# Sums one at a time, and one line of product steps across block borders, in a fused attention and SwiGLU kernel

## The chip, the cores and the metric

The kernel runs on one core of one Trainium2 chip. Time is device time in microseconds (us) of one execution. Before the change the median of 13 runs is 353.88 us, from 352.03 to 356.42.

## The reference

Sliding-window attention with an ALiBi bias feeds a SwiGLU block. The attention has 8 batches, 8 heads, 576 positions, 64 values per head and a window of 128. Its output is laid out as a matrix x of 4608 tokens by 512. Then:

```
attn = softmax(scale * q @ k.T + bias, masked to the window) @ v
x    = attn, as [4608, 512]
g    = x @ w_gate                     # [4608, 1536]
h    = g * sigmoid(g) * (x @ w_val)   # [4608, 1536]
out  = h @ w_out                      # [4608, 512]
```

Inputs and output are float32; the kernel computes its products in float16 with float32 sums.

## The kernel before, in words

**Blocks.** The tokens go in nine blocks (0 to 8) of 512. A block's x is held transposed (`xT`, four chunks of 128 rows by 512 tokens), and so is its h (`hT`, twelve chunks of 128 rows by 512 tokens). Attention runs beside blocks 0 to 5 and is finished before block 6, so blocks 6 to 8 and the tail hold only the SwiGLU part. The change lies there.

**h @ w_out by seven products.** `strassen(n, t)` computes the output of block n for one half of its tokens, t = 0 or 1, as a 2x2 block product with seven multiplications instead of eight (the Winograd form). Its operands are quarters of `hT` and three sums of them, S2, S3 and S4 (a fourth sum, S1, is written over a quarter of `hT`). Each of the seven steps is one product of six matmuls (line 525), followed by a copy on ScalarE or by a scaled add into an output row (`osb`) on VectorE (line 529). The 14 steps of a block, t = 0 and then t = 1, are called p0 to p13 here. The third and tenth (p2, p9) read S2, the fifth and twelfth (p4, p11) S3, the sixth and thirteenth (p5, p12) S4. S2, S3 and S4 have one buffer each (pool `sp`). The accumulators X and Y of a `strassen` are the two halves of one PSUM tile with one buffer.

**The sums of h.** `sums(n, c)` makes a third of S2, S3 and S4, from the chunks of units c and c + 3, in four operations on VectorE: S3, the in-place add, S2, S4 (lines 492 to 495).

**Gate and value by seven products.** For blocks 6 to 8 (`SEVEN_FROM` is 6) `gate_val_by_seven(n)` computes gate and value with the same form. It works on six units of 256 gate columns each. A unit has seven steps, named first to seventh, each a product of four matmuls (line 617). On PSUM tiles X, Y and Z: first starts X, and ScalarE copies it to Z; fifth starts Y (copied as p5); sixth adds to X (copied as u2); second adds to Z, and ScalarE takes its silu; third adds to Y, VectorE adds u2 (line 653) and multiplies into `hT` (line 654); seventh adds to X, VectorE adds p5 (line 660), which gives v; fourth adds to X after that, ScalarE takes its silu (line 667), and VectorE multiplies it with v into `hT` (line 668). X and Y come from a pool of four PSUM banks. x has sums too: `x_sums(n)` makes three of them and one in place (lines 600 to 603), in halves of the masks' memory that attention has left.

**Order of the steps.** A unit's steps are mixed with those of the unit ahead of it:

```
for step, of in ((first, u), (seventh, u - 1), (fifth, u), (sixth, u), (fourth, u - 1),
                 (second, u), (third, u)):
```

The loop runs to u = 6, so the last unit's seventh and fourth come alone at the end of the block, before the next block begins. After every third step one h product of the block before is put in (`parts`). After the last block, `ends` emits the fourteen h products of block 8 in a written order.

**What sets the order on the engines.** From step 198 of the emission on, TensorE runs in the order in which the program is written; VectorE's and ScalarE's order is chosen by a planner from its own estimates, and each runs its queue in that order. SP's queue holds the transposes of x and the stores of output rows; POOL's queue holds the loads, all done by then.

Of the kernel before, what the change touches and what calls it, by code (L numbers as in the profile page):

```python
# [31 lines left out]
SEVEN_FROM = 6  # L32
SILU_AT = 7
# [18 lines left out]
def kernel(  # L52
# [10 lines left out]
    nc = tc.nc  # L63
# [4 lines left out]
    NMB = DFF // P  # L68
    NSUP = B // 2
    NBLK = NTOK // 512  # L70
# [93 lines left out]
    units = [(s, p) for s in range(NSUP) for p in range(9)]  # L164
# [265 lines left out]
    def gate_val(n, m):  # L430
        c0 = 384 if (n, m) in acted else 0
        gate(n, m, wide(n, m, "g"), c0)
        yield
        val(n, m, wide(n, m, "v"), c0)
        yield
# [45 lines left out]
    one_more = []  # L481
    hsum = {}

    def sums(n, c):

        if n not in hsum:
            hsum[n] = [spool.tile([P, HM, 256], FP16, name=f"S{i}", tag=f"S{i}") for i in (2, 3, 4)]
        lo, hi = slice(2 * c, 2 * c + 2), slice(HM + 2 * c, HM + 2 * c + 2)
        a11, a12 = hT[n][:, lo, 0:256], hT[n][:, hi, 0:256]
        a21, a22 = hT[n][:, lo, 256:512], hT[n][:, hi, 256:512]  # L490
        s2, s3, s4 = (t_[:, lo, :] for t_ in hsum[n])
        nc.vector.tensor_sub(s3, a11, a21)
        nc.vector.tensor_add(a21, a21, a22)
        nc.vector.tensor_sub(s2, a21, a11)
        nc.vector.tensor_sub(s4, a12, s2)

    def strassen(n, t):

# [75 lines left out]
    G1, G2 = wg_sb[:, 0:HK, :], wg_sb[:, HK:NKB, :]  # L574
    V1, V2 = wv_sb[:, 0:HK, :], wv_sb[:, HK:NKB, :]
# [10 lines left out]
    def gate_val_weight_sums(u):  # L586

        cols = slice(2 * u * P, (2 * u + 2) * P)
        t1, t2, t3, t4 = tsum[u] = t_homes[4 * u:4 * u + 4]
        nc.vector.tensor_sub(t1, V1[:, :, cols], G1[:, :, cols])  # L590
        nc.vector.tensor_sub(t3, V2[:, :, cols], V1[:, :, cols])
        nc.vector.tensor_sub(t2, V2[:, :, cols], t1)
        nc.vector.tensor_sub(t4, G2[:, :, cols], t2)

    def x_sums(n):

        a11, a12 = xT[n][:, 0:HK, 0:256], xT[n][:, HK:NKB, 0:256]
        a21, a22 = xT[n][:, 0:HK, 256:512], xT[n][:, HK:NKB, 256:512]
        s2, s3, s4 = xsum[n] = spare[3 * (n % 2):3 * (n % 2) + 3]
        nc.vector.tensor_sub(s3, a11, a21)  # L600
        nc.vector.tensor_add(a21, a21, a22)
        nc.vector.tensor_sub(s2, a21, a11)
        nc.vector.tensor_sub(s4, a12, s2)

    def gate_val_by_seven(n):

        x = xT[n]
        A11, A12 = x[:, 0:HK, 0:256], x[:, HK:NKB, 0:256]
        S1, A22 = x[:, 0:HK, 256:512], x[:, HK:NKB, 256:512]
        S2, S3, S4 = xsum.pop(n)  # L610
        hT[n] = hpool.tile([P, NMB, 512], FP16, name="hT", tag="hT")
        live = {}

        def product(dst, w, c0, a, start=False):
            for i in range(2):
                for kb in range(HK):
                    nc.tensor.matmul(dst[:, i, :], w[:, kb, c0 + i * P:c0 + (i + 1) * P], a[:, kb, :],  # L617
                                     start=(start and i == 0 and kb == 0),
                                     stop=(i == 1 and kb == HK - 1), skip_group_check=True)

        def first(u):
            X, Y = (ps_a.tile([P, 2, 256], FP32, name=i, tag="a", bufs=4) for i in ("gX", "gY"))
            Z = ps_f.tile([P, 2, 256], FP32, name="gZ", tag="gv")
            live[u] = X, Y, Z
            product(X, G1, 2 * u * P, A11, True)
            nc.scalar.copy(Z, X)

        def fifth(u):
            Y = live[u][1]
            product(Y, tsum[u][0], 0, S1, True)  # L630
            p5 = epool.tile([P, 2, 256], FP32, name="p5", tag="exc", bufs=5)
            nc.scalar.copy(p5, Y)
            live[u] += (p5,)

        def second(u):
            Z = live[u][2]
            product(Z, G2, 2 * u * P, A12)
            s = supool.tile([P, 2, 256], FP16, name="s1", tag="tt")
            nc.scalar.activation(s, Z, AF.Silu)
            live[u] += (s,)  # L640

        def sixth(u):
            X = live[u][0]
            product(X, tsum[u][1], 0, S2)
            u2 = epool.tile([P, 2, 256], FP32, name="u2", tag="exc", bufs=5)
            nc.scalar.copy(u2, X)
            live[u] += (u2,)

        def third(u):
            X, Y, Z, p5, u2, s = live[u]  # L650
            product(Y, V2, 2 * u * P, S4)
            v_ = supool.tile([P, 2, 256], FP16, name="v1", tag="uu")
            nc.vector.tensor_add(v_, Y, u2)
            nc.vector.tensor_mul(hT[n][:, 2 * u:2 * u + 2, 0:256], s, v_)

        def seventh(u):
            X, Y, Z, p5, u2, s = live[u]
            product(X, tsum[u][2], 0, S3)
            v_ = supool.tile([P, 2, 256], FP16, name="v2", tag="uu")
            nc.vector.tensor_add(v_, X, p5)  # L660
            live[u] = X, v_

        def fourth(u):
            X, v_ = live.pop(u)
            product(X, tsum[u][3], 0, A22)
            s = supool.tile([P, 2, 256], FP16, name="s2", tag="tt")
            nc.scalar.activation(s, X, AF.Silu)  # L667
            nc.vector.tensor_mul(hT[n][:, 2 * u:2 * u + 2, 256:512], s, v_)  # L668

        last_u = NMB // 2  # L670
        for u in range(last_u + 1):
            for step, of in ((first, u), (seventh, u - 1), (fifth, u), (sixth, u), (fourth, u - 1),
                             (second, u), (third, u)):
                if 0 <= of < last_u:
                    step(of)
                    if step is fourth and of >= last_u // 2:
                        sums(n, of - last_u // 2)
                    yield step

    AT = {2, 3, *range(5, 10), *range(11, 18)}  # L680

    def ffn():

        for n in range(NBLK):
            if n > 1:
                parts = chain(strassen(n - 1, 0), strassen(n - 1, 1))
            if n == 1:
                for j in range(PRE):
                    for _ in project(0, j, ps_f, "po", 1):
                        yield 1.0  # L690
            if n >= SEVEN_FROM:
                k = 0
                for k, _ in enumerate(gate_val_by_seven(n)):
                    if n == SEVEN_FROM and k in (3, 10, 17):
                        gate_val_weight_sums(3 + k // 7)
                    yield 0.5
                    if k % 3 == 1 and next(parts, 0) is None:
                        yield 0.75
                    if k == 36 and n + 1 < NBLK:
                        x_sums(n + 1)  # L700
                assert next(parts, 0) == 0
                continue
            for m in range(NMB):
                for half, _ in enumerate(gate_val(n, m)):
                    yield 1.0
                    if n > 1 and 2 * m + half in AT:
                        next(parts)
                        yield 0.75
                if n == 1:
                    if m in (4, 6, 8, 10):  # L710
                        for _ in project(0, m // 2 - 2, ps_f, "po", 1):
                            yield 1.0
                    if m in (4, 6, 8):
                        weight_sums(m // 2 - 2)
                if n > 0 and m >= 9:
                    sums(n, m - 9)
                if n + 1 == SEVEN_FROM:
                    if m == SILU_AT:
                        attention_ends()
                        by_silu.update((n, i) for i in range(m + 1, NMB))  # L720
                    if m in (SILU_AT + 1, SILU_AT + 2):
                        gate_val_weight_sums(m - SILU_AT - 1)
                    if m == NMB - 1:
                        gate_val_weight_sums(2)
                        x_sums(n + 1)
            if n > 1:
                assert next(parts, 0) == 0

        ends = [strassen(NBLK - 1, t) for t in range(2)]
        for t in (0, 1, 0, 1, 0, 0, 0, 1, 0, 0, 1, 1, 1, 1):  # L730
            next(ends[t])
            yield 0.75

# [220 lines left out]
```

## Time and profile before

| | |
|---|---|
| median of 13 runs | 353.88 us |
| lowest, highest | 352.03, 356.42 us |
| the profiled execution: its time, its span | 354.86 us, 353.1 us |
| TensorE busy, matmuls | 336.1 us (95%), 2983 |
| VectorE busy, instructions | 277.6 us (79%), 652 |
| ScalarE busy, instructions | 207.1 us (59%), 412 |
| mean granted TensorE clock | 0.990 |
| block 6 begins; last product of block 8's fourth begins | 249.19 us; 339.43 us |

The page has the busy time of each engine, the span in 40 slices of 8.83 us with the busy share of each in tenths, and groups of instructions by line. Besides it the trace answers who waited for whom, and lists the instructions of one engine in order of time. In such a list a line has the start in us, the duration in us, the engine, the line of the kernel, the operation, and output<-input with shapes; a wait before it stands in brackets with the instruction that ended it. PE is TensorE, DVE is VectorE, ACT is ScalarE. Line numbers are those of the kernel before.

### The profile page before, as it was taken

To read this page: it belongs to the slowest core of one execution; us is meant where nothing else is said; L and a number is where in the kernel's file an instruction comes from. 1 tells how busy PE (TensorE), PEld (TensorE's weight loads), DVE (VectorE), ACT (ScalarE), POOL (GpSimd) and SP (SyncE) were. 2 spreads that over 40 slices of the span, in tenths; PEclk is the share of its full clock that TensorE was granted. 3 is DMA by queue.
4 is the path that set the end of the run, shared out by engine and by line. 5 is a ranking of instruction groups with operands and counts; after the bars stand their busy time and mean duration, and the time that the engine had idled before them with its cause. 6 is when DMAs were issued, how large, how long until landed. Compare 5 with 4: busy or idle time off the path is not lost.

```text
span 353.1 us, 7803 instructions
## 1 busy us (share of the span) xinstructions
PE 336.1 (95%) x2983; PEld 221.0 (63%) x2983; DVE 277.6 (79%) x652; ACT 207.1 (59%) x412; POOL 108.2 (31%) x134
## 2 busy tenths in 40 slices
PE   7999989999999999999999999999999799799975
PEld 3584445444456655666566655566788688688864
DVE  5568886999787799778998999999756955845673
ACT  2758773566555756656556554474666567476630
POOL 8966584348485564545310000000000000000000
PEclk9999998999999999999999999999999999989999
DMA  9999999999999999999995032123010101101014
GB/s 151 170 180 186 141 183 161 93 141 130 141 166 179 155 180 158 178 142 188 170 125 106 18 90 17 42 64 90 2 61 0 61 3 59 62 0 61 0 61 120
DMA packets 158981, 37.37 MB, mean 106 GB/s; under 512 B 147296, under 2 KB 154592, under 8 KB 158944
## 3 DMA queue, kind: packets, MB, share of 16 engines
q0 software_dynamic: 117280, 18.62, 77.9%
q1 hardware_dynamic: 40976, 17.64, 28.0%
q10 hardware_dynamic: 688, 0.62, 0.6%
q8 instruction: 23, 0.38, 0.5%
q14 instruction: 14, 0.11, 0.1%
HBM read 37.91 MB, written 9.44 MB: 134 GB/s over the span
## 4 chain that ended last, share of the span: by engine, by line
PE 70%; DVE 18%; ACT 4%; DMA 4%; issue 3%; POOL 0%; ACTq 0%; DVEq 0%
PE po L525 14%; PE pg L398 13%; PE pv L398 13%; PE gX L617 7%; PE gY L617 4%; PE ps L279 4%; PE av L346 3%; PE po L452 3%; DMA qn<-in_q_dram 3%; PE p L525 3%; DVE hT L428 2%; DVE uu L417 2%; PE gZ L617 2%; ACT ex L285 2%; PE pt L222 1%
## 5 line engine op out<-in xcount | busy, mean ns | idle before, releaser
L398 PE MATMUL pv<-xT,wv_sb 128*128 128x512 f16 (+2 forms) x320 | 76.8, 358 | 0.4 <-DVE hT L428 0.2
L398 PE MATMUL pg<-xT,wg_sb 128*128 128x512 f16 (+2 forms) x320 | 76.2, 358 | 0.4 <-DVE hT L428 0.2
L416 ACT ACTIVATE tt<-pg 128x512 f16<-128x512 f32 (+2 forms) x70 | 41.5, 592 | 39.6 <-PE pg L398 39.0
L285 ACT ACTIVATE ex<-ps 128x512 f16<-128x512 f32 x96 | 50.5, 606 | 16.3 <-PE ps L279 16.3
L417 DVE SCALAR_TENSOR_TENSOR uu<-tt,pg 128x512 f16<-128x512 f16 (+2 forms) x69 | 45.9, 665 | 11.1 <-ACT tt L416 11.0
L428 DVE TENSOR_TENSOR hT<-uu,pv 128x512 f16<-128x512 f16 (+2 forms) x70 | 46.5, 664 | 3.4 <-PE pv L398 1.8
L398 PEld LDWEIGHTS <-wg_sb 128*128 128x128 f16 x320 | 28.5, 98 | 25.2 <-issue 3.5
L525 PEld LDWEIGHTS <-hT 128*128 128x128 f16 x384 | 36.9, 99 | 11.4 <-issue 3.0
L398 PEld LDWEIGHTS <-wv_sb 128*128 128x128 f16 x320 | 28.5, 98 | 24.5 <-issue 2.7
L191 POOL DMA_DIRECT2D kn<-in_k_dram x39 | 33.3, 857 | 33.1 <-DMA kT<-kn 24.8
L191 POOL DMA_DIRECT2D qn<-in_q_dram x39 | 33.3, 858 | 24.5 <-DMA qT<-qn 7.6
L185 POOL DMA_DIRECT2D va<-in_v_dram x40 | 34.1, 858 | 21.7 <-PE av L346 16.9
L291 DVE TENSOR_TENSOR ex<-ex,m_reg 128x1024 f16<-128x1024 f16 x42 | 28.8, 687 | 5.6 <-ACT ex L285 5.4
L525 PEld LDWEIGHTS <-S 128*128 128x128 f16 x288 | 27.5, 98 | 7.6 <-issue 1.8
L349 DVE TENSOR_TENSOR x<-av,rec 128x256 f16<-128x256 f32 x72 | 28.8, 419 | 0.5
L525 PE MATMUL po<-T,hT 128*128 128x256 f16 x192 | 26.2, 273 | 1.4 <-DVE osb L529 1.4
L668 DVE TENSOR_TENSOR hT<-s,v 128x512 f16<-128x512 f16 x18 | 7.6, 423 | 24.7 <-ACT s L667 24.7
L525 PE MATMUL po<-T,S 128*128 128x256 f16 x192 | 26.1, 273 | 0.3 <-ACT p5s L553 0.3
L318 ACT ACTIVATE exc<-psc 128x512 f16<-128x512 f32 x40 | 21.4, 610 | 7.6 <-PE psc L314 7.6
L346 PEld LDWEIGHTS <-ex 128*128 128x128 f16 x384 | 17.8, 98 | 5.2 <-issue 0.9
L346 PE MATMUL av<-va,ex 128*128 128x65 f16 x384 | 19.7, 194 | 0.3
L279 PE MATMUL ps<-qT,kT 64*128 64x256 f16 x192 | 18.4, 272 | 0.6 <-DVE osb L529 0.2
(134 smaller groups left out, 540.8 us busy)
## 6 DMA issues: line engine op xcount, KB each, us to landing
out_dram<-osb SPq DMA_DIRECT2D x32, 256.0 KB, 2.4
va<-in_v_dram POOLq DMA_DIRECT2D x32, 128.0 KB, 9.3
qn<-in_q_dram POOLq DMA_DIRECT2D x31, 128.0 KB, 7.6
kn<-in_k_dram POOLq DMA_DIRECT2D x31, 128.0 KB, 7.7
wo_sb<-in_moe_w_out_dram POOLq DMA_DIRECT2D x2, 768.0 KB, 9.7
wg_sb<-in_moe_w_gate_dram POOLq DMA_DIRECT2D x4, 256.0 KB, 7.9
wv_sb<-in_moe_w_val_dram POOLq DMA_DIRECT2D x4, 256.0 KB, 8.3
wg_sb<-in_moe_w_gate_dram POOLq DMA_DIRECT2D x1, 512.0 KB, 9.2
```

What stands on the lines that cost most here:

```text
L185: nc.gpsimd.dma_start(va[rank][p0:p1, :, 0:D], src)
L191: nc.gpsimd.dma_start(t_[p0:p1], src)
L279: nc.tensor.matmul(two[par][:, j, :], kT[rows, ks, pair, :], qT[rows, p:p + 2, pair, :], start=(j == 0 and not early_tile), stop=(j == 1))
L285: nc.scalar.activation(e[:, o:o + 2, :], banks[q4][par], AF.Exp, scale=scale)
L291: nc.vector.tensor_mul(e[:, o, :], e[:, o, :], reg[:, o, :])
L346: nc.tensor.matmul(av[:, j, :], w, val, start=(n == 0), stop=(n == len(todo) - 1))
L398: nc.tensor.matmul(ps[:, c0:c1], w[:, kb, ms], xT[n][:, kb, c0:c1], start=(kb == 0 and c0 == 0), stop=(kb == NKB - 1 and c1 == 512), skip_ ...
L416: nc.scalar.activation(tt, pg[:, c0:c1], AF.Tanh, scale=0.5)
L417: nc.vector.scalar_tensor_tensor(out=uu, in0=tt, scalar=one if (n, m) == PIN else 1.0, in1=pg[:, c0:c1], op0=ALU.add, op1=ALU.mult)
L428: nc.vector.tensor_mul(hT[n][:, m, c0:c1], acted[(n, m)][1][:, c0:c1], pv[:, c0:c1])
L525: nc.tensor.matmul(dst, a[:, m, cols], b[:, m, :], start=(start and m == 0), stop=(m == HM - 1), skip_group_check=True)
L617: nc.tensor.matmul(dst[:, i, :], w[:, kb, c0 + i * P:c0 + (i + 1) * P], a[:, kb, :], start=(start and i == 0 and kb == 0), stop=(i == 1 an ...
```

## The change

The sums of h, of x and of the weights are no longer emitted in fours on the spot. The functions return lists of single operations; in blocks 6 to 8 these go into a list `later`, from which one or two are emitted behind each product step. Outside of that stretch `at_once` emits them as before. The sums of x for the next block are put on the list at step 20 of a block instead of behind step 36.

The steps of the three blocks' eighteen units form one line, `seven_steps`. A block's last unit does its seventh and fourth between the steps of the next block's first unit. In the last unit of block 8, seventh comes behind second, and the first h product of the tail is put behind it. The h products of a block are counted from its step 0, one behind every third step; those of block 6's predecessor begin at the same count.

```diff
+    def four_sums(a11, a12, a21, a22, s2, s3, s4):
+
+        return [lambda: nc.vector.tensor_sub(s3, a11, a21),
+                lambda: nc.vector.tensor_add(a21, a21, a22),
+                lambda: nc.vector.tensor_sub(s2, a21, a11),
+                lambda: nc.vector.tensor_sub(s4, a12, s2)]
+
+    def at_once(fs):
+        for f in fs:
+            f()
+
     def sums(n, c):
 ...
-        nc.vector.tensor_sub(s3, a11, a21)
-        nc.vector.tensor_add(a21, a21, a22)
-        nc.vector.tensor_sub(s2, a21, a11)
-        nc.vector.tensor_sub(s4, a12, s2)
+        return four_sums(a11, a12, a21, a22, s2, s3, s4)
 ...
-        last_u = NMB // 2
-        for u in range(last_u + 1):
-            for step, of in ((first, u), (seventh, u - 1), (fifth, u), (sixth, u), (fourth, u - 1),
-                             (second, u), (third, u)):
-                if 0 <= of < last_u:
-                    step(of)
-                    if step is fourth and of >= last_u // 2:
-                        sums(n, of - last_u // 2)
-                    yield step
+        return {f.__name__: f for f in (first, second, third, fourth, fifth, sixth, seventh)}
+
+    def seven_steps():
+
+        units = [(n, u) for n in range(SEVEN_FROM, NBLK) for u in range(NMB // 2)]
+        of = {}
+        for i, (n, u) in enumerate(units):
+            if u == 0:
+                of[n] = gate_val_by_seven(n)
+            now, before = (n, u), units[i - 1] if i else None
+            if i + 1 < len(units):
+                turn = (("first", now), ("seventh", before), ("fifth", now), ("sixth", now),
+                        ("fourth", before), ("second", now), ("third", now))
+            else:
+                turn = (("first", now), ("seventh", before), ("fifth", now), ("sixth", now),
+                        ("fourth", before), ("second", now), ("seventh", now), ("third", now),
+                        ("fourth", now))
+            for k, (name, which) in enumerate(turn):
+                if which is not None:
+                    of[which[0]][name](which[1])
+                yield n, 7 * u + k, name, which
 ...
-            if n >= SEVEN_FROM:
-                k = 0
-                for k, _ in enumerate(gate_val_by_seven(n)):
-                    if n == SEVEN_FROM and k in (3, 10, 17):
-                        gate_val_weight_sums(3 + k // 7)
-                    yield 0.5
-                    if k % 3 == 1 and next(parts, 0) is None:
-                        yield 0.75
-                    if k == 36 and n + 1 < NBLK:
-                        x_sums(n + 1)
-                assert next(parts, 0) == 0
-                continue
+            if n == SEVEN_FROM:
+                break
 ...
         ends = [strassen(NBLK - 1, t) for t in range(2)]
-        for t in (0, 1, 0, 1, 0, 0, 0, 1, 0, 0, 1, 1, 1, 1):
+        final = ()
+        for n, k, name, which in seven_steps():
+            if k == 0 and n > SEVEN_FROM:
+                assert next(parts, 0) == 0
+                parts = chain(strassen(n - 1, 0), strassen(n - 1, 1))
+            if n == SEVEN_FROM and k in (3, 10, 17):
+                later.extend(gate_val_weight_sums(3 + k // 7))
+            yield 0.5
+            if k % 3 == 1 and k < 42:
+                next(parts)
+                yield 0.75
+            if k == 20 and n + 1 < NBLK:
+                later.extend(x_sums(n + 1))
+            if k == 35:
+                later.extend(sums(n, 0))
+            if name == "fourth" and which is not None and which[1] > 3:
+                if which == (NBLK - 1, 5):
+                    at_once(final)
+                else:
+                    later.extend(sums(which[0], which[1] - 3))
+            if n == NBLK - 1 and k == 40:
+                final = sums(n, 2)
+                later.append(final.pop(0))
+            for _ in range(2 if len(later) > 4 or k >= 39 or k < 7 else 1):
+                if later:
+                    later.pop(0)()
+            if n == NBLK - 1 and k == 41:
+                next(ends[0])
+                yield 0.75
+        assert next(parts, 0) == 0 and not later
+
+        for t in (1, 0, 1, 0, 0, 0, 1, 0, 0, 1, 1, 1, 1):
             next(ends[t])
             yield 0.75
```

More of the change, by code (lines that the diff above doesn't have):

```diff
@@ L589, in gate_val_weight_sums @@
         t1, t2, t3, t4 = tsum[u] = t_homes[4 * u:4 * u + 4]
[L590 to L593, printed above, removed]
+        return [lambda: nc.vector.tensor_sub(t1, V1[:, :, cols], G1[:, :, cols]),
+                lambda: nc.vector.tensor_sub(t3, V2[:, :, cols], V1[:, :, cols]),
+                lambda: nc.vector.tensor_sub(t2, V2[:, :, cols], t1),
+                lambda: nc.vector.tensor_sub(t4, G2[:, :, cols], t2)]
     def x_sums(n):
@@ L599, in x_sums @@
         s2, s3, s4 = xsum[n] = spare[3 * (n % 2):3 * (n % 2) + 3]
[L600 to L603, printed above, removed]
+        return four_sums(a11, a12, a21, a22, s2, s3, s4)
+    later = []
     def gate_val_by_seven(n):
@@ L649, in third @@
         def third(u):
-            X, Y, Z, p5, u2, s = live[u]
+            X, Y, Z, p5, u2, s = live[u][:6]
             product(Y, V2, 2 * u * P, S4)
@@ L660, in seventh @@
             nc.vector.tensor_add(v_, X, p5)
-            live[u] = X, v_
+            live[u] += (v_,)
         def fourth(u):
-            X, v_ = live.pop(u)
+            X, v_ = live[u][0], live[u][-1]
+            del live[u]
             product(X, tsum[u][3], 0, A22)
@@ L715, in ffn @@
                 if n > 0 and m >= 9:
-                    sums(n, m - 9)
+                    at_once(sums(n, m - 9))
                 if n + 1 == SEVEN_FROM:
@@ L721, in ffn @@
                     if m in (SILU_AT + 1, SILU_AT + 2):
-                        gate_val_weight_sums(m - SILU_AT - 1)
+                        at_once(gate_val_weight_sums(m - SILU_AT - 1))
                     if m == NMB - 1:
-                        gate_val_weight_sums(2)
-                        x_sums(n + 1)
+                        at_once(gate_val_weight_sums(2))
+                        at_once(x_sums(n + 1))
             if n > 1:
```

## The prediction

> **What bounds the kernel now.** I read the page's shares first, then the waits of the stretch that the change touches (249 to 353.1 us, blocks 6 to 8 and the tail), then the two engines' timelines at a border between blocks.
>
> The page, shares and slices:
>
> ```profile
> PE 336.1 (95%) x2983; PEld 221.0 (63%) x2983; DVE 277.6 (79%) x652; ACT 207.1 (59%) x412; POOL 108.2 (31%) x134
> ...
> PE   7999989999999999999999999999999799799975
> PEld 3584445444456655666566655566788688688864
> DVE  5568886999787799778998999999756955845673
> ```
>
> TensorE is the bound, full except in slices 31, 34 and 38. Those lie where block 6, 7 and 8 end, and VectorE is at 9, 8 and 7 there against 4 to 6 in the middle of a block. The waits of the stretch, as us in total, times, longest:
>
> ```profile
> DVE hT L668 <- ACT s L667: 24.7, 14, 2.0
> ...
> PE gX L617 <- DVE v L660: 4.2, 3, 1.4
> ...
> PE po L525 <- DVE osb L529: 1.4, 3, 0.5
> ```
>
> TensorE waits six times in 104 us, twice at each of three places, always for VectorE. The first line says that VectorE has slack inside a block (up to 2.0 us per unit), so only the borders cost. TensorE's timeline at the end of block 6, and VectorE's beside it:
>
> ```profile
> 274.74 0.60 PE L617 MATMUL gY<-m_reg,wv_sb 128*128 128x256 f16 x4
> 275.17 0.60 PE L617 MATMUL gX<-m_reg,m_c 128*128 128x256 f16 x4
> 276.22 0.81 PE L525 MATMUL po<-T,hT 128*128 128x256 f16 x6 [0.45 <-DVE osb L529]
> 278.43 0.60 PE L617 MATMUL gX<-xT,m_c 128*128 128x256 f16 x4 [1.39 <-DVE v L660]
> 278.86 0.60 PE L617 MATMUL gX<-xT,wg_sb 128*128 128x256 f16 x4
> ```
>
> ```profile
> 271.01 0.69 DVE L653 TENSOR_TENSOR v<-gY,u 128x512 f16<-128x512 f32 x1 [0.42 <-PE gY L617]
> ...
> 275.76 0.41 DVE L529 SCALAR_TENSOR_TENSOR osb<-po,u2s 128x256 f32<-128x256 f32 x1
> ...
> 277.69 0.68 DVE L660 TENSOR_TENSOR v<-gX,p 128x512 f16<-128x512 f32 x1
> ```
>
> An x product (4 matmuls) takes 0.437 us from start to start (275.17 less 274.74), an h product (6 matmuls) 0.656. So seventh of unit 5 ends at 275.61 and the h product starts 0.61 late; that one ends at 276.88 and fourth starts 1.55 late. Together 2.16 us. VectorE runs without a gap from 271.01 to 278.7, and the v that fourth waits for is only reached at 277.69. Blocks 7 and 8 repeat both waits (305.89 and 308.09; 337.23 and 339.43), so the borders hold 3 x 2.16 = 6.48 us. After block 7 there is more:
>
> ```profile
> 308.09 0.95 PE L617 MATMUL gX<-xT,m_c 128*128 128x256 f16 x4 [1.39 <-DVE v L660]
> 308.83 1.06 PE L617 MATMUL gX<-xT,wg_sb 128*128 128x256 f16 x4
> 309.69 1.06 PE L617 MATMUL gY<-xT,kT 128*128 128x256 f16 x4
> 310.54 1.35 PE L525 MATMUL po<-wo_sb,hT 128*128 128x256 f16 x6
> 311.72 0.60 PE L617 MATMUL gX<-m_reg,kT 128*128 128x256 f16 x4
> ```
>
> The same four products took 278.43 to 280.39, 1.96 us, after block 6, and 3.63 us here: 1.67 us lost to a slower clock, at one border of three.
>
> [...] while fourth waits, nothing behind it runs. [...] seventh's result was there at about 275.8, and v was reached at 277.69. [...] two gaps of 0.61 and 1.55 us were enough once, and not enough twice.
>
> **The change, part by part.** No instruction is added or removed on any engine; the queues of SP and POOL keep their order, so no DMA moves.
>
> Single sums. TensorE alone is ordered by hand here; VectorE's order is the planner's. At a border it is nearly what it was: the same 17 operations stand between v of third(4) and v of seventh(5), three S3 sums still together. I cost this part alone at nothing. What is new: the first half of an output row (osb from p5s) moves ahead of two of them, and add, S2 and S4 of the last group are now mixed with the next block's v.
>
> One line across borders. Now fourth(5) comes three steps behind seventh(5), as inside a block, with p0, fifth and sixth of the next block between. The h products move one place against the unit's steps, one in every three steps as before. I went through the waits inside a block. The tightest are a copy or output row (0.2 us after the product, 0.34 to 0.60 long) against three steps (1.31 us) to its next user, and fourth, which needs v of seventh within 1.53 us and gets it after 0.2 + 0.7. The trace shows no wait for the same pairs today. Cost nothing; without that cover about 0.4 us for each of 18 units.
>
> Now the border. I count from the end of third(4), 270.81 in the trace. TensorE without a stall: p11 to 0.66, first(5) 1.09, seventh(4) 1.53, fifth 1.97, p12 2.62, sixth 3.06, fourth(4) 3.50, second 3.93, p13 4.59, third(5) 5.03, next first 5.46, seventh(5) 5.90, p0 6.56, fifth 6.99, sixth 7.43, and fourth(5) is due. VectorE needs the same 6.68 us as in the trace (271.01 to 277.69), from 0.20: v begins at 6.88, and with its 0.68 and 0.05 for the signal TensorE goes on at 7.62. A stall of **0.19**. p13 is due at 3.93; the osb that it waits for starts about 3.1 and ends at 3.6, so the 0.61 goes.
>
> What is late next is p2 of the next block, which reads S2. In the kernel before, S2's last third was ready at 281.25 and used at about 284.1. Now p2 follows fourth(5) after p1, second, third and first: 0.656 + 3 x 0.437 = 1.97 us, and its fifth weight load is the first to read the last third, at 10.47 with the 0.19. VectorE at the border 6 to 7: v 6.88 to 7.48, then the four x sums that the planner puts here (0.45 each, since each waits for the last) until 9.2, hT of fourth (silu ends at fourth's end + 0.83 = 8.89) 9.2, osb 9.5, add 9.85, v of the next third 10.2, S2 from 10.8 to 11.2. Stall **0.80**. Border 7 to 8 has no x sums: hT 8.89, osb 9.23, add 9.56, v 9.90, S2 10.50 to 10.92, stall **0.51**. Behind p2 wait seventh and fifth of the new block, and nothing else is late.
>
> The tail. Unit 5 has no next block, so seventh(5) moves up behind p13 and one of the tail's products behind it. v now stands one v, one sum and one product earlier: it begins at 5.59 and ends at 6.28, fourth is due at 6.12, stall **0.22**. Three h products instead of four lie before S2's first user: due at 9.19, S2 ends at 9.22, **0.09**.
>
> Sum: 6.48 - (0.19 + 0.80) - (0.19 + 0.51) - (0.22 + 0.09) = **4.5 us** less. Against the profiled execution, 354.86: 350.4. If the border's clock drop goes with the stall, another 1.67: 348.7. The median, 353.88, is 0.98 lower; 13 runs spread over 4.4 us while the border stalls repeat to 0.01, so I read the spread as more or fewer clock drops, and give the median run 0.6 us of them at borders. 353.88 - 4.5 - 0.6 = **348.8**.
>
> Bounds of what the trace doesn't show: the two S2 waits, 0 (if the planner's order leaves more slack than I count) to 1.5 each (if v or silu come 0.7 later); I take 0.80 and 0.51, counted from measured pitches. The clock: 0 to 3 drops of 1.67 are saved, or one new one is bought.
>
> **The rivals.**
> VectorE keeps up: no stall left at the borders. All of 6.48 and the clock share: 346.8. For it, up to 2.0 us of slack per unit; against it, the dense stretch from 271.01 to 278.7 keeps its operations and order.
> The lag only moves: VectorE is the bound at a border, and p2 takes most of what fourth gives. If S2 comes 0.8 later than I count at each of the three places and the clock drops stay, the gain is 4.5 - 2.4 = 2.1: 351.8. For it, the waits computed above; against it, 2 us of slack in the very next unit.
> The change doesn't do what it says: the planner undoes the single emission, as its order already shows. Then the second part alone acts, which is the forecast, not another time.
> Slower: p2 becomes a worse place to wait than fourth was. Place: the last third of S2, three x products behind fourth(5). Each us by which it comes later than I count costs a us at each border. At 1.5 us later (S2 waits of 2.3, 2.0 and 1.6) the 4.5 are gone, at 2.1 the kernel is 1.8 slower: 355.7. 1.5 us is five more sums (0.34) or three more v (0.60) in front of S2; the order has none, so only late inputs (silu, p5) could do it.
>
> **How the numbers follow.** Forecast 0.56 (own range 347.2 to 350.6), VectorE keeps up 0.18, the lag moves 0.18, slower 0.08. The range from 346.3 to 352.3 leaves out the slow case and the outer ends. A measurement of this kernel tells about 0.5% from no change, 1.8 us. Faster by that (under 352.1): the first two and over half of the third, 0.85; within it the rest of the third, 0.08; slower 0.07.
>
> **What would show it.** Right: fourth's wait for v at 0.0 to 0.4, three times; the wait of the h product for osb gone; a new wait of TensorE for the S sum behind the borders after block 6 and 7, the first longer; slices 31, 34 and 38 of TensorE at 9 nearly throughout; matmul counts unchanged. Wrong: waits of TensorE inside blocks, for a copy or for osb; S2 waits over 1.5; or half-clock stretches at places where there were none.

## The result, and the profile after

The changed kernel takes **348.91 us** (median of 11 runs, 348.0 to 349.35) against 353.93 for the kernel before beside it (48 runs, 351.96 to 356.63). The ratio is 0.985, with a 95% interval from 0.9825 to 0.987: faster by 1.5%. The profiled execution took 349.35 us, its span 347.6.

The page of the changed kernel, shares and slices (a slice is 8.69 us here):

```profile
PE 333.9 (96%) x2983; PEld 219.4 (63%) x2983; DVE 277.5 (80%) x652; ACT 207.4 (60%) x412; POOL 108.2 (31%) x134
...
PE   7999988999999999999999999999999999999995
...
PEclk9999999999999999999999999999999999999999
```

The numbers of instructions are the same. Counted from 0 as in the prediction, TensorE's slices stand at 9 from slice 7 to slice 38: the three dips of before (slices 31, 34 and 38) are filled. From the first product of block 6 to the last product of the tail it was 99.21 us (249.19 to 348.40) and is 93.55 (249.25 to 342.80).

Who waits for whom in that stretch, as us in total, times, longest:

```profile
DVE hT L676 <- ACT s L675: 21.4, 13, 1.9
...
PEld L533 <- DVE S L488: 1.8, 3, 0.9
PE po L533 <- DVE S L488: 1.0, 2, 0.6
PE gX L624 <- DVE v L667: 0.6, 3, 0.2
```

Lines have moved: 624 is the x product, 533 the h product, 667 seventh's v, 488 the sum S2. TensorE's wait for an output row (`osb`) is gone. Its wait for v has shrunk from 4.2 to 0.6, and the sum S2 is a new releaser, seen by the weight load first and then by the product behind it. This view counts from the listed end of a product (277.85 + 0.60 below, which leaves 0.17), so I measure waits as before, from the pitch of the products (0.437, which leaves 0.33). The changed kernel's TensorE at the border after block 6:

```profile
277.85 0.60 PE L624 MATMUL gX<-m_reg,kT 128*128 128x256 f16 x4
278.62 0.60 PE L624 MATMUL gX<-xT,m_c 128*128 128x256 f16 x4 [0.17 <-DVE v L667]
279.06 0.82 PE L533 MATMUL p<-wo_sb,hT 128*128 128x256 f16 x6
279.71 0.60 PE L624 MATMUL gZ<-xT,wg_sb 128*128 128x256 f16 x4
280.15 0.60 PE L624 MATMUL gY<-m_c,wv_sb 128*128 128x256 f16 x4
280.59 0.60 PE L624 MATMUL gX<-xT,wg_sb 128*128 128x256 f16 x4
281.02 0.60 PE L533 MATMUL po<-T,S 128*128 128x256 f16 x4
282.27 0.39 PE L533 MATMUL po<-T,S 128*128 128x256 f16 x2 [0.65 <-DVE S L488]
```

Fourth of unit 5 comes at 278.62, 0.33 after the end of sixth (277.85 + 0.437). Then p1, second, third and first of the new block run without a gap, and p2 stops before its fifth matmul: four matmuls from 281.02 end at 281.46, the fifth starts at 282.27, 0.81 late. After block 7 the same two are 0.34 and 0.50, in the tail 0.37 and 0.10. Together 2.45 us where 6.48 stood, and no other product waits between 249 and 343 us.

The chain of waits of the changed kernel, cut to that border, says who holds the end here:

```profile
277.97 0.60 DVE v L667
278.57 0.34 DVE m_reg L486
...
280.20 0.42 DVE hT L676
280.61 0.33 DVE osb L548
280.95 0.33 DVE hT L487
281.28 0.60 DVE v L660
281.88 0.34 DVE S L488
282.22 0.05 issue
282.27 0.39 PE po L533 x2
```

After block 6 VectorE works off its queue without a gap, with x sums (lines 486 to 489) between v and the multiply, and TensorE starts 0.05 us after S2's last third. The lag of VectorE is still there. What changed is that TensorE has other work while it lasts.

After block 7, where no x sums stand in the queue, the second wait has a longer chain. VectorE is idle before the multiply until fourth's silu is there:

```profile
306.55 0.68 DVE L667 TENSOR_TENSOR v<-gX,p 128x512 f16<-128x512 f32 x1
308.55 0.43 DVE L676 TENSOR_TENSOR hT<-s,v 128x512 f16<-128x512 f16 x1 [1.32 <-ACT s L675]
```

So a late v delays fourth, fourth its silu, and the silu the multiply and all that stands behind it in VectorE's queue, up to S2 at 310.16. Half an output row and a v, 0.34 and 0.60 us, stand in that queue ahead of S2, which needs neither. An estimate from these starts: without them, and with 0.45 us from each of the dependent operations to the next, S2 would start at 309.45, 0.7 us sooner, where TensorE waits 0.50. That was not tried.

### The profile page after: what moved, and what is told of

Read it like the earlier page. It is cut to its first block, busy times and chain, and to the rows that moved or that the text cites. A ratio compares the mean times of both kernels' runs of the same rounds, so it can differ in the third digit from the quotient of the medians.

```text
span 347.6 us, 7798 instructions
## 1 busy us (share of the span) xinstructions
PE 333.9 (96%) x2983; PEld 219.4 (63%) x2983; DVE 277.5 (80%) x652; ACT 207.4 (60%) x412; POOL 108.2 (31%) x134
## 4 chain that ended last, share of the span: by engine, by line
PE 59%; DVE 17%; DMA 11%; POOL 4%; issue 4%; ACT 4%; POOLq 0%; ACTq 0%; DVEq 0%
PE po L533 13%; PE pg L398 12%; PE pv L398 11%; PE gX L624 6%; DMA va<-in_v_dram 3%; DMA wo_sb<-in_moe_w_out_dram 3%; PE gY L624 3%; PE av L346 3%; DMA wv_sb<-in_moe_w_val_dram 3%; PE ps L279 2%; PE p L533 2%; DVE hT L428 2%; PE po L452 2%; DMA qn<-in_q_dram 2%; DVE uu L417 2%
```

## The experiments

Besides the changed kernel itself, each kernel is an edit of it. "Stretch" is from the first product of block 6 to the last product of the tail in the profiled run: 93.55 us for the changed kernel, and 93.54 in a second profile of it.

### One part alone: the line without the single sums

```diff
-                later.extend(gate_val_weight_sums(3 + k // 7))
+                at_once(gate_val_weight_sums(3 + k // 7))
...
-            if k == 20 and n + 1 < NBLK:
-                later.extend(x_sums(n + 1))
...
-                    later.extend(sums(which[0], which[1] - 3))
...
+            if k == 36 and n + 1 < NBLK:
+                at_once(x_sums(n + 1))
+            if name == "fourth" and which is not None and which[1] > 2:
+                at_once(sums(which[0], which[1] - 3))
```

> The changed kernel, but with the sums emitted in fours on the spot again, so that only the one line of steps is left. Theory (the line alone does it, since the planner orders VectorE whatever the emission is): the order of TensorE and ScalarE is that of the changed kernel, VectorE's differs in some twenty places at each border; fourth's waits sum to about 0.4 us a border, S2's to 0.8 and 0.5; 348.9, within 0.4 of the changed kernel. Rival (the single emission spreads VectorE's work and carries a part of the gain): 350 or more, with fourth's wait over 1 us.

Measured: 349.09 us (6 runs, ratio 0.985, 0.981 to 0.990). So the line alone brings nearly everything. Its stretch was 94.41, though, 0.86 more, and its trace has a wait that the changed kernel doesn't have. TensorE of this kernel:

```profile
271.28 0.60 PE L624 MATMUL gY<-xT,qT 128*128 128x256 f16 x4
272.12 0.81 PE L533 MATMUL po<-wo_sb,S 128*128 128x256 f16 x6 [0.24 <-DVE osb L537]
```

and VectorE beside it:

```profile
270.65 0.42 DVE L486 TENSOR_TENSOR S<-hT 128x512 f16<-128x512 f16 x1
270.98 0.42 DVE L661 TENSOR_TENSOR hT<-s,v 128x512 f16<-128x512 f16 x1
271.32 0.42 DVE L487 TENSOR_TENSOR hT<-hT 128x512 f16<-128x512 f16 x1
271.65 0.42 DVE L537 SCALAR_TENSOR_TENSOR osb<-po,p5s 128x256 f32<-128x256 f32 x1
```

p12 waits 0.40 us for the half output row, since S3 and the in-place add stand ahead of it. In the changed kernel that row (271.76) comes directly behind v. The wait repeats at each border (0.40, 0.41, 0.41), while fourth waits 0.21, 0.21 and 0.25 instead of 0.33 to 0.37, and S2's waits are the same: 3.30 us in all against 2.45. The medians of 348.91 and 349.09 did not show that, so both kernels ran once more, side by side.

> The changed kernel once more, beside the kernel with the one line alone, so that the two stand against the same runs of the kernel before. If the single sums are worth what the waits of the two traces say (3.30 less 2.45 us, 0.85), it is 0.5 to 1.1 us below that kernel in the median. If the planner's order makes it up elsewhere, the two are within 0.3 us.

> The one line alone once more (sums in groups of four, as in the kernel before). By the waits of its trace 0.85 us above the changed kernel, about 349.7 if that is at 348.9. If the single sums are worth nothing, within 0.3 us of it.

Measured: 348.41 for the changed kernel, 349.79 for the line alone (6 runs each, the kernel before 353.44 beside them); stretches of 93.54 and 94.41. Over all runs of each the medians are 348.43 (17 runs) and 349.49 (12). The single sums are worth about 0.9 us, given the line.

### The other part alone: single sums in the old order of steps

```diff
-        units = [(n, u) for n in range(SEVEN_FROM, NBLK) for u in range(NMB // 2)]
...
+        for u in range(last_u + 1):
+            for step, of in ((first, u), (seventh, u - 1), (fifth, u), (sixth, u), (fourth, u - 1),
+                             (second, u), (third, u)):
...
+                    if step is fourth and of >= last_u // 2:
+                        later.extend(sums(n, of - last_u // 2))
```

> The kernel before, with its order of steps, but with the sums put on a list and emitted singly behind the steps. Theory (the line alone does it): TensorE waits 2.0 to 2.3 us at each of the three block ends for osb and v, as before; 353.9, within 0.7 of the kernel before. Rival (the single emission carries a part): 352 or less and the block ends' waits under 1.5 us.

Measured: 353.92 us (22 runs), ratio 1.002 (0.999 to 1.004), no change. The waits of this kernel's TensorE for v:

```profile
PE gX L624 <- DVE v L667: 5.4, 3, 1.9
```

By pitch the borders hold 0.28 + 1.88, 0.28 + 2.09 and 0.27 + 1.88 us, 6.68 against 6.48 before. The half row comes earlier and p13 waits 0.33 less, and fourth waits 0.33 or 0.54 more: VectorE's queue up to v is no shorter. Here an operation moved ahead at a border paid nothing, since TensorE had nothing to do before what it was moved ahead of.

### The tail as before

```diff
-            if i + 1 < len(units):
-                turn = (("first", now), ("seventh", before), ("fifth", now), ("sixth", now),
-                        ("fourth", before), ("second", now), ("third", now))
-            else:
-                turn = (("first", now), ("seventh", before), ("fifth", now), ("sixth", now),
-                        ("fourth", before), ("second", now), ("seventh", now), ("third", now),
-                        ("fourth", now))
+            turn = (("first", now), ("seventh", before), ("fifth", now), ("sixth", now),
+                    ("fourth", before), ("second", now), ("third", now))
+            if i + 1 == len(units):
+                turn += (("seventh", now), ("fourth", now))
```

with block 7's last h product between seventh and fourth again, and the fourteen products of `ends` in their old order.

> The changed kernel, but the end of block 8 as in the kernel before: seventh, an h product and fourth of the last unit alone at the end, and the tail's old order. Theory (each border gives its own stall back, independently): one wait of fourth for v of about 2.0 us at the end in place of 0.47 us of two waits, the other two borders as in the changed kernel; 1.6 us slower than the changed kernel, 350.5. Rival (the gain sits mostly in clock drops that the two inner borders caused): within 0.5 of the changed kernel.

Measured: 350.24 us (6 runs), 1.33 above the changed kernel, stretch +1.25. The waits after blocks 6 and 7 stayed (fourth 0.34 and 0.34, S2 0.80 and 0.51), and in the tail fourth waits 1.72 where 0.37 and 0.10 stood:

```profile
333.82 0.60 PE L624 MATMUL gX<-xT,m_c 128*128 128x256 f16 x4 [1.56 <-DVE v L667]
```

The tail's wait came back alone, and the stretch grew by what that wait says.

### A dose of lateness for S2

```diff
-        return four_sums(a11, a12, a21, a22, s2, s3, s4)
+        fs = four_sums(a11, a12, a21, a22, s2, s3, s4)
+        return fs[:3] + fs[2:3] * 3 + fs[3:] if c == 2 and n >= SEVEN_FROM else fs
```

> The changed kernel with the subtraction that makes the last third of S2 written three more times behind itself (the same values) in blocks 6 to 8. Theory (TensorE waits at the borders for VectorE's queue up to S2's last third, and pays one for one): the last copy lands about 1.5 us later; S2's waits grow from 0.81, 0.50 and 0.10 to about 2.3, 2.0 and 1.5, sum +4.5, 353.4; and since the gaps are as long as in the kernel before, clock drops and a spread of over 2 us come back. Rival (the wait for S2 hides behind something else that is late): waits grow by less than 0.5 each, 350 or less.

Measured: 354.84 us (20 runs), ratio 1.004 (1.001 to 1.006): slower than before the change. The S2 waits are 2.40, 2.10 and 1.68, so 1.59, 1.60 and 1.58 were added, 4.77 in all. But the median rose by 5.9, or by 6.4 from that of all 17 runs of the changed kernel. TensorE of this kernel, after block 6:

```profile
283.69 0.39 PE L534 MATMUL po<-T,S 128*128 128x256 f16 x2 [2.24 <-DVE S L488]
...
284.36 0.60 PE L625 MATMUL gY<-xT,kT 128*128 128x256 f16 x4
284.79 0.88 PE L625 MATMUL gX<-m_reg,kT 128*128 128x256 f16 x4
285.47 1.48 PE L534 MATMUL po<-T,hT 128*128 128x256 f16 x6
286.75 1.06 PE L625 MATMUL gX<-xT,kT 128*128 128x256 f16 x4
```

Within 1.5 us of the wait's end the products run at half rate (0.85 us from 286.75 to the next instead of 0.437): the clock drop that the profile of before shows at one border is back, here after the wait for S2, and it comes again after block 7. The granted clock of this run was 0.70 from 286 to 290 us and 0.72 from 313 to 319. The stretch of this profile is 101.67 us, 8.12 more than that of the changed kernel: 4.77 of added waits, and 1.66 and 1.65 of products at the lower rate. 15 of the 20 runs had a mean clock of 0.995 or less, against 1 of 17 for the changed kernel. So drops come with the longer stall, here one for another operation than before. The five runs with a mean clock of 0.998 or more have a median of 353.71, so the clock is 1.1 of the 1.2 to 1.6 us beyond the added waits.

### VectorE in the order of emission

Does the planner undo the single emission? Here VectorE too runs in the written order from step 198.

```diff
-ENGINES = {"all": None, "compute": {ET.PE, ET.DVE, ET.Activation}, "pe": {ET.PE}}
+ENGINES = {"all": None, "compute": {ET.PE, ET.DVE, ET.Activation}, "pe": {ET.PE}, "two": {ET.PE, ET.DVE}}
...
-                fixed.enter_context(tc.manual_schedule(engines=ENGINES["pe"]))
+                fixed.enter_context(tc.manual_schedule(engines=ENGINES["two"]))
```

> The changed kernel with VectorE's order also taken from the emission from step 198 on, so that the single sums stand where the text puts them. Theory (VectorE is late by what it has to do at a border, whatever the order): each sum now stands directly behind the one that it needs, 0.45 us each instead of 0.34, and v of seventh comes later; fourth's wait 0.8, S2's 0.4 at each border; 349.3. Rival (the planner is what spoils the single emission): all border waits under 0.3, 347 or less.

Measured: 356.34 us (6 runs), ratio 1.008 (1.006 to 1.011); the expectation of the time missed. The borders came close to it (fourth 0.88, 0.88, 1.05; S2 0.49, 0.50, none in the tail), but there is a new wait at block 6's start:

```profile
252.53 0.61 PE L624 MATMUL gY<-xT,kT 128*128 128x256 f16 x4 [3.40 <-DVE xT L487]
```

In the written order the sums of the weights stand ahead of block 6's own x sums, and fifth of its first unit waits 3.6 us for the in-place one; the planner had moved the x sums up. Behind that wait the products run at the lower rate for a while (four matmuls in 0.85 us from 254.30 to 255.15), which costs another 1.5 us, and 0.5 to 1.0 us more is lost at three places inside blocks. So the emission, taken literally for all of VectorE, is no gain. How much of the loss the sums have in it was not separated from VectorE's other operations.

### Where the rest sits: h products later, x sums earlier

Two edits for the two waits that are left. One puts each h product a step later, so that p2 stands behind one more x product of the new block; the other gives block 8's x sums memory of their own, so that they don't have to wait for block 6's readers.

```diff
-            if k % 3 == 1 and k < 42:
+            if k % 3 == 2 and k < 42:
```

> The changed kernel with each h product put one step later (behind steps 2, 5, 8 and so on of a block). Theory (what is left of the stalls is VectorE being late by a fixed amount at the borders): p2 gets 0.44 us more until its last third of S2, and v has one more step too; fourth's wait falls from 0.33 to under 0.1, S2's from 0.81 and 0.50 to under 0.4 and 0.1; 1.5 to 2 us faster than the changed kernel, 347.1. Rival (VectorE's lag moves with the products, since the planner orders anew): the sum of waits stays near 2.4 us, 348.9.

Measured: 348.1 us (6 runs), stretch 92.95, 0.60 less; 347.1 had been expected. At the first two borders fourth's waits are gone and S2's are 0.10 and nothing, as foreseen, but VectorE is late again for fourth of the next block's first unit:

```profile
283.26 0.60 PE L624 MATMUL gX<-xT,kT 128*128 128x256 f16 x4 [0.60 <-DVE v L667]
```

It waits 0.76 after block 6, 0.42 after block 7, and p1 in the tail 0.42.

```diff
-        s2, s3, s4 = xsum[n] = spare[3 * (n % 2):3 * (n % 2) + 3]
+        own = [nat.tile([P, HK, 256], FP16, name="own", tag="kn") for _ in range(3)] if n == NBLK - 1 else None
+        s2, s3, s4 = xsum[n] = own or spare[3 * (n % 2):3 * (n % 2) + 3]
```

> The changed kernel with the sums of x for block 8 in memory of their own (left over from attention's loads), so that the planner can do them before block 6 instead of at the border from block 6 to 7. Theory (the four x sums stand in front of S2 there and make the difference between 0.81 and 0.50): the first S2 wait falls to 0.50, all else as in the changed kernel; 0.3 faster, 348.6. Rival: the wait stays at 0.8, since silu of fourth is the late input; 348.9.

Measured: 348.42 us (4 runs), stretch 93.26. The planner puts those four sums at the start of block 6 (248.1 to 252.2 us), and the S2 wait after that block falls from 0.81 to 0.51, about the value after block 7:

```profile
280.76 0.39 PE L533 MATMUL po<-T,S 128*128 128x256 f16 x2 [0.35 <-DVE S L488]
```

So 0.30 us of that border was the x sums, as the prediction's two counts of it differ. The medians don't show it (348.42 with four runs, 348.43 for the changed kernel); the traces do. Both edits together:

> Both: h products one step later, and the x sums of block 8 in memory of their own. With the h products later the waits for S2 are gone and what is left is a wait of the next unit's fourth, 0.76 us at the first border and 0.42 at the second. Theory (that is VectorE's lag, passed on, and the x sums are in it at the first border): 0.76 falls to about 0.4; 0.35 us faster than with the h products later alone, 347.7. Rival (the wait is the order's own): stays at 0.76, 348.1.

Measured: 347.66 us (4 runs), ratio 0.984 (0.9815 to 0.987), and once more beside the changed kernel:

> The h products one step later and the x sums of block 8 in memory of their own, once more. By the stretch of its trace (92.64 against 93.55 us) 0.9 us below the changed kernel; by the medians so far 1.2. If these were only chance, within 0.3 us of it.

Measured: 347.5 us (6 runs) against 348.41 for the changed kernel, 0.9 less; the stretch, 92.62, is 0.92 less. It is the best of the kernels here. What it still waits for, after block 6 (the 0.76 is now 0.42):

```profile
283.27 0.60 PE L625 MATMUL gX<-xT,kT 128*128 128x256 f16 x4 [0.26 <-DVE v L668]
```

This is no longer a queue that is behind all along. VectorE is idle for 1.17 us before fourth's multiply at 279.80, which waits for the silu, and is busy without a gap from there to this v.

## Why the prediction was right, step by step

**The borders' waits are what the line takes away.** Right. With the singles alone 6.68 us of them stay and the time doesn't move; with the line alone the time falls by nearly all of it.

**p13's wait goes, nothing waits inside a block.** Right: TensorE has six waits in the stretch, two at each border and two in the tail.

**Fourth's waits of 0.19, 0.19 and 0.22.** 0.33, 0.34 and 0.37; the mechanism was right and the count of VectorE's work 0.14 short. Here is VectorE of the changed kernel from the end of third of unit 4 (270.87) on:

```profile
270.82 0.42 DVE L676 TENSOR_TENSOR hT<-s,v 128x512 f16<-128x512 f16 x1 [1.90 <-ACT s L675]
271.16 0.68 DVE L660 TENSOR_TENSOR v<-gY,u 128x512 f16<-128x512 f32 x1
...
275.37 0.41 DVE L676 TENSOR_TENSOR hT<-s,v 128x512 f16<-128x512 f16 x1
275.82 0.43 DVE L487 TENSOR_TENSOR hT<-hT 128x512 f16<-128x512 f16 x1
276.28 0.42 DVE L488 TENSOR_TENSOR S<-hT 128x512 f16<-128x512 f16 x1
276.62 0.68 DVE L660 TENSOR_TENSOR v<-gY,u 128x512 f16<-128x512 f32 x1
...
277.89 0.68 DVE L667 TENSOR_TENSOR v<-gX,p 128x512 f16<-128x512 f32 x1
```

The prediction let v begin 0.20 after the product. It begins 0.29 after, because the multiply of the fourth before it, late from ScalarE, is still running; that is 0.09. From there to the last v it is 6.73 us, not 6.68. The 17 operations are the same in number, but the multiply, the in-place add and S2 now follow each other directly, and each uses what the one before it writes: they start 0.45 and 0.46 apart, where others of that shape start 0.335 apart. The "same 6.68 us" held one such pair (v and its multiply, 0.79 instead of 0.60), the new order two. For these operations a dependence costs about 0.115 us: 0.335 from start to start without one (275.03 to 275.37), 0.45 with one.

**S2's waits of 0.80, 0.51 and 0.09.** 0.81, 0.50 and 0.10, and the 0.30 between the first two is the x sums, as the run that moves them shows. The 0.14 that fell short at fourth delays both sides of this count, TensorE behind fourth and VectorE before S2, and cancels.

**The single sums at nothing.** This step of the prediction was wrong, by 0.87 us, though not for the sums alone: without the line they are worth nothing (353.92). Beside the line they spare p12 a wait of 0.40 at each border and cost fourth 0.12. The prediction saw the half row move ahead of two sums and gave it no price. Since it took its count from the new order, which has the row in front, the total didn't suffer; the split between the two parts did.

**The clock.** The drop after block 7 went with the stall, 1.67 us in the profiled execution: 99.21 less 4.03 of waits less 1.67 makes 93.51, and 93.55 was measured. In the median 0.6 was too little. Of 63 runs of the kernel before, beside the experiments, 27 have a mean clock of 0.998 or more and a median of 352.41, and the median of all is 353.69: 1.28 us. These drops need not all lie at borders. The profiled execution of before has a second one in attention, where the change does nothing (granted clock 0.55 from 52 to 54 us and 0.60 from 54 to 56, as from 308 to 310 and 310 to 312). That most of them go with the change is seen from the kernels, not from the single runs: 36 of 63 runs of before have a mean clock of 0.995 or less, and 1 of 17 of the changed kernel.

**The sum.** Waits gave 4.03 instead of 4.5, the clock 1.3 instead of 0.6, so the median came out at 348.9 and 348.4 with 348.8 forecast: two errors of opposite sign. The way to the forecast was right; that it came within 0.4 us was in part luck. The kernel before at full clock (352.41) and the changed kernel, all of whose runs but one have a mean clock of 0.997 or more (348.43), stand 3.98 us apart, which is the waits' 4.03.

**The rivals.** That VectorE keeps up is not so in this kernel: 2.45 us of waits for it remain. That the lag only moves isn't either, though it does move. The argument put against it, 2 us of slack in the next unit, was too generous: with the h products a step later that unit's fourth waits, though after block 7 VectorE was idle for 1.18 us before fourth's multiply. What comes behind a late silu is dense enough to be late itself. The slower rival exists at the place named, and its rate was right for the waits (1.59 us later each, 4.77 in all). Its turning point was set too late. The dose of 1.59 gave 1.15 us more than before (354.84 to 353.69 beside it), where the prediction's own sum would have given 0.3. By pitch this kernel waits 7.24 us against 6.48 before, 0.76 more, since fourth's waits are 0.46 above their count. The clock doesn't make the difference: it takes 1.1 us from the median of this kernel and 1.28 from that of before. The rest, 0.4, is within the interval of the ratio. That the planner undoes the single emission fell with the p12 wait.

## What to carry to other kernels

Where an engine that is not the bound falls behind at a loop's border, count its queue, in order, up to the operation that the bound engine needs, with dependent neighbours at their longer distance (0.45 us against 0.335 here), and give the bound engine work of the next block in that time. Then count on to the next thing that is read, along the whole chain: a late product makes a late silu, and all that stands behind its multiply in the queue is late with it, needed or not (after block 7 VectorE stood idle for 1.32 us before that multiply, and TensorE waited 0.50 for S2). A stall's price here was its own length plus what the clock lost behind it (4.77 us of added waits and 3.31 of slower products in the profile of the dose), and the second was seen in the spread of the runs sooner than in one profile.

## What the runs showed of the hardware

**More of the runs have a lower clock in the kernels with the longer stalls of TensorE.** The share of runs with a mean granted clock of 0.995 or less, by the stalls in the kernel: 36 of 63 before (0.61 and 1.55 us within 2.8 us, at three places); 15 of 22 with 0.28 and 1.88 to 2.09; 15 of 20 with 0.33 to 0.37 and 1.68 to 2.40; 5 of 6 with 3.56 at block 6's start and eight more of 0.47 to 1.05; 0 of 6 with a single 1.72 in the tail; 4 of 49 in the kernels whose stalls are at most 0.81. Of the kernel before, 31 runs with a mean clock from 0.993 to 0.995 have a median of 354.43 and 5 at 0.990 or less one of 356.37, so 2.0 us above the full-clock runs and 1.9 above that. In the profile of before the products behind the border after block 7 ran at half rate (four matmuls in 0.86 us from 308.83 to 309.69 instead of 0.437, granted clock 0.55 from 308 to 310 us) after 2.15 us of idleness within 2.8 us, and over half of that kernel's runs have such a mean clock. How long a stall it takes was not shown. Why it strikes in one run and not in the next was not tried, and for runs without a profile the place of the drop isn't known; one of the two drops in the profile of before is not at a border.

**Two VectorE operations that depend on each other** start 0.45 us apart at 128x512 in float16 (275.37 to 275.82), 0.11 more than two that don't (275.03 to 275.37), and the addition whose operand is read from PSUM takes 0.60 to the next start (271.16 to 271.76), or 0.79 when its reader follows directly (271.01 to 271.80 in the kernel before).
